# Staircase products, sums of groups and logits of an attention kernel moved into one step at one tile size, and output transposes moved beside those of keys

## The chip, the cores and the metric

The kernel runs on one core of a Trainium2 chip (trn2). The metric is the device time of one execution in microseconds (us). The core has a matrix engine (PE, with its weight loads shown apart as PEld), a vector engine (DVE), a scalar or activation engine (ACT), a general engine (POOL) and a queue engine that issues most transfers (SP). Each engine takes its instructions strictly in the order of the program; engines wait for each other by semaphores.

## The reference, cut to what matters

```python
# attention, B=4, H=8, S=768, D=64, fp32; block 32, window 16
k_sum = k.reshape(B, H, nb, block, D).max(axis=3)      # 24 group keys
v_sum = v.reshape(B, H, nb, block, D).mean(axis=3)     # 24 group values
scores_l = scale * q @ k.T            # kept only where |i - j| < window
scores_s = scale * q @ k_sum.T + log(block)
a = softmax(concat([scores_l, scores_s]))
attn = a @ concat([v, v_sum])
# then x = attn as 3072 tokens of 512, a two-level top-1 router (4 groups of 4
# experts) and the chosen expert's relu(x @ w1) @ w2, weighted
```

## The kernel before, in words

The attention is done in 16 "pairs" (one batch, two heads; 4 batches of 4 pairs), each in three steps g0, g1, g2 of four query tiles of 64 rows; the loop over `n` runs 48 such steps and three more that drain it. The mixture of experts follows; its time is most of the run, and its first parts begin as soon as the last logits are there.

What a step issues, and in which order, is written out by hand in the table `PLAN` (L47 to L49), one list for each of g0, g1, g2. All engines take their instructions in that order:

- `s`, `e`: scores of the step (16 matmuls of 64x64 tiles into `ps_s`, then DVE adds the mask and takes the maximum into `ss` and `nm`, L747), and ACT's exponentials `pr` (L756). `e` of a step needs its `ss`.
- `t`, `v`: transposes of `pr` two steps old (PE, 128x128, into `ps_tr`; ACT copies `ptS`, L764) and, three steps old, products with the values `va` (PE, 128x64, into `ps_av`); DVE then makes the reciprocal `rs` (L778) and the output `xt` (L779).
- `p0` to `p4`: preparation of the next pair. `p0` and `p1` transpose the keys of its two heads (`kn`, PE, 128x128); of each, ACT copies one half into `kw` and DVE the other (both L716; for the pairs that `ACT_K1` names, 10 to 15, ACT copies both halves of the second head). `p2`, `p3` transpose the queries (`qn`), and ACT copies `qt` (L710, two copies each). `p4` is DVE alone: two copies of window edges inside `kw` (L724, L725), the maximum over groups `ks` (L727) and its copy into `kw` (L730). The scores of the next pair's g0 come behind it.
- `m0`, `m1`: group means of the values. `m0` is 12 matmuls with the matrix `stair`, which write four groups of 32 rows of a bank, so that the tile of the array is 64x32; DVE copies the result to `vp` (L683). `m1` is one matmul with `same` (128x32); DVE copies it to `vr` (L687), and POOL spreads it over the 12 tiles of `va` in six copies (L690). The next pair's `v` needs them. In PLAN `m0` works for the pair after the current one and `m1` for the current one.
- `l0` to `l3`: logits of a finished pair. `l0` transposes four tiles of `xt` (ACT copies `xT`), `l1` the last two (DVE copies `xT`; both L800), `l2` multiplies with `wcat` (128x32, into `ps_lg`), `l3` is DVE's part once in a batch. `l0` runs one pair behind, `l1` to `l3` two.

All transposes, `m0` and `m1` take their result bank from one ring, `ps_tr`, of three banks: each new use waits until the copy out of the third one before it has ended. Where the table puts a step therefore also sets which copy it waits for. From step 17 on, DVE work of the router (`ROUTE_AT`) is dealt out between DVE's instructions. Transfers of q, k, v are issued from SP one to three pairs ahead.

`qt`, `kw`, `va`, `vp` and `xT` name the tiles in all rows below; every matmul and transpose is recorded at L118, a helper, so that PE's instructions are told apart by their tiles.

Of the kernel before, what the change touches and what calls it, by code (L numbers as in the profile page):

```python
# [8 lines left out]
F32 = mybir.dt.float32  # L9
# [12 lines left out]
B, H, S, D = 4, 8, 768, 64  # L22
# [6 lines left out]
NBLK = S // BLOCK  # L29
QT = 64  # L30
RUN = 8
NQT = S // QT

KW = QT + 2 * PAD
# [9 lines left out]
EPS = 1e-9  # L44
NEG = -1.0e9

PLAN = [["s", "p0", "t", "p1", "v", "m1", "l1", "e", "p4"],  # L47
        ["s", "p2", "t", "v", "l2", "e"],
        ["s", "p3", "l3", "t", "v", "m0", "l0", "e"]]  # L49
LAG = {"l0": 1, "l1": 2, "l2": 2, "l3": 2}  # L50

T_LAG, V_LAG = 2, 3
# [33 lines left out]
class Clock:  # L86

    pe, dve = float("-inf"), 0.0
    step = 0
# [452 lines left out]
def attention(tc, q, k, v, w_group, w_expert, ident, x_dram, ps, router, hook):  # L542
# [24 lines left out]
    with ExitStack() as st, ExitStack() as nat_st:  # L567
        cst = st.enter_context(tc.tile_pool(name="a_cst", bufs=1))
# [5 lines left out]
        order = [(b, a) for b in range(B) for a in range(NP)]  # L574
# [35 lines left out]
        t = ps_lg.next()  # L610
# [16 lines left out]
        def init_last(i):  # L627

            nc.gpsimd.memset(va_ring[i][96:NR, :, :, 0:D], 0.0)
# [33 lines left out]

        stair = cst.tile([QT, 2 * NBLK + 6], F32, name="stair")
        V.memset(stair, 0.0)
        for i in range(2):
            V.memset(stair[BLOCK * i:BLOCK * i + BLOCK, NBLK - 2 + i:NBLK - 1 + i], 1.0 / BLOCK)
# [3 lines left out]
        def means(idx, part):  # L673

            va = va_ring[idx % NVA]
            t = ps_tr.next()
            if part == 0:
                for i in range(NQT):
                    j = i % 4
                    T.matmul(out=t[32 * j:32 * j + 32, 0:P], lhsT=stair[:, NBLK - 2 - 2 * i:NBLK + 30 - 2 * i],  # L680
                             rhs=va[0:QT, i, :, 0:D], start=(i < 4), stop=(i >= NQT - 4), skip_group_check=True)
                vps[idx] = sm.tile([P, P], F32, name="vp", bufs=2)
                V.tensor_copy(out=vps[idx], in_=t[:, 0:P])  # L683
            else:
                T.matmul(out=t[KW:NC, 0:P], lhsT=same, rhs=vps.pop(idx), start=True, stop=True)
                vr = wk.tile([NC, 1, 2, D], F32, name="vr")
                V.tensor_copy(out=vr[KW:NC].rearrange("p a h d -> p (a h d)"), in_=t[KW:NC, 0:P])  # L687
                n = 2
                for i in range(0, NQT, n):
                    nc.gpsimd.tensor_copy(out=va[KW:NC, i:i + n, :, 0:D], in_=vr[KW:NC].broadcast_to([NBLK, n, 2, D]))  # L690
# [41 lines left out]
        def scores(n):  # L732

            idx, g = n // 3, n % 3
            qt, kw = qts[idx % 2], kws[idx % 2]
            sp = [ps_s.next()[:, 0:2 * NC].rearrange("p (j c) -> p j c", j=2) for _ in range(2)]
            for j in range(2):
                for i, h in ((0, 0), (1, 1), (1, 0), (0, 1)):
                    t, rows = 4 * g + 2 * j + i, slice(64 * h, 64 * h + 64)
                    T.matmul(out=sp[h][64 * i:64 * i + 64, j], lhsT=qt[rows, t].rearrange("p j r -> p (j r)"),  # L740
                             rhs=kw[rows, t], start=True, stop=True, skip_group_check=True)
            nm = sm.tile([P, 4], F32, name="nm")
            ss = sm.tile([P, 4, NC], F32, name="ss", bufs=2)
            for h in range(2):
                for j in range(2):
                    u, t = 2 * h + j, 4 * g + 2 * j
                    V.tensor_tensor_reduce(out=ss[:, u], in0=mask[:, 1 if t == 0 else 2 if t == NQT - 2 else 0],  # L747
                                           in1=sp[h][:, j], scale=1.0, scalar=3.4e38, op0=ALU.add, op1=ALU.min,
                                           accum_out=nm[:, u:u + 1])
            advance(OPS["s"][g])  # L750
            return ss, nm

        def exps(n, sp, nm):
            pr = prr[n % 3]
            for i in range(4):
                nc.scalar.activation(out=pr[:, i, 0:NC], in_=sp[:, i], func=AF.Exp, bias=nm[:, i:i + 1], scale=-1.0)  # L756
            return pr

        def transpose_p(pr):
            pt = ps_tr.next()  # L760
            for i in range(4):
                T.transpose(out=pt[0:NR, i * P:(i + 1) * P], in_=pr[:, i], identity=ident)
            ptS = wk.tile([NR, 4, P], F32, name="ptS", bufs=3)
            nc.scalar.copy(out=ptS.rearrange("p a c -> p (a c)"), in_=pt[0:NR])  # L764
            return ptS
# [20 lines left out]
        def store():  # L786
            b, js = stores.pop(0)
            nc.sync.dma_start(out=x_dram[b * S:(b + 1) * S].rearrange("(j r) d -> r j d", r=P)[:, js], in_=xs[b][:, js])
# [52 lines left out]
        for n in range(NG + 3):  # L841
            idx, g = n // 3, n % 3
            if n < NG:
                b, a = order[idx]
                xs[b] = x_ring[b % 2]
            for step in PLAN[g]:
                if step == "s" and n < NG:
                    sps = scores(n)
                elif step == "e" and n < NG:
                    prs[n] = exps(n, *sps)  # L850
                elif step == "t" and 0 <= n - T_LAG < NG:
                    pts[n - T_LAG] = transpose_p(prs.pop(n - T_LAG))
                elif step == "v" and 0 <= n - V_LAG < NG:
                    values((n - V_LAG) // 3, (n - V_LAG) % 3, pts.pop(n - V_LAG))
                elif step[0] == "p" and n < NG and idx + 1 < len(order):
                    prep(idx + 1, int(step[1]))
                elif step[0] == "m" and n < NG:
                    j = idx + (step == "m0")
                    if 0 < j < len(order):
                        means(j, int(step[1]))  # L860
                elif step[0] == "l" and 0 <= idx - LAG[step] < len(order):
                    logits(idx - LAG[step], int(step[1]))
            if n == 0:
                for i in range(1, NVA):
                    init_last(i)
                router.consts()
            elif n < 3:
                means(0, n - 1)
            if n in ROUTE_AT:
                b1 = ROUTE_AT.index(n)  # L870
                work.append(router.route(b1 * TB, (b1 + 1) * TB))
                if b1 == 1:
                    work.append(router.first_blocks())
            if n == NG - 4:
                nat_st.close()
            if n < NG:
                if g == 0 and 0 < idx < len(order) - 3:
                    qk[idx + 3] = load_qk(idx + 3)
                if g == 0 and idx + 2 < len(order):
                    load_vw(idx + 2)  # L880
            if g == 1 and stores:
                store()
            while stores and n == NG - 5:
                store()
            clock.step += 1
            hook(n, need, w1_first)
# [422 lines left out]
```

## Time and profile before

| | |
|---|---|
| median of 3 runs | 574.27 us (572.64 to 576.89) |
| profiled execution, own time | 573.17 us |
| span in its profile | 571.5 us |
| PE, DVE, ACT, POOL busy | 92%, 66%, 59%, 22% of the span |
| attention loop, first g2 of the pairs at | 17.85 us (pair 0) to 174.65 us (pair 14) |

In the rows a line of the timeline is start, busy time, engine, line of the code, operation, output tile<-input tiles, shape of output<-input and how many instructions the row joins; in brackets the idle time of the engine ahead of it and what ended it. A line of windows gives, for a stretch, its length and the busy time of each engine with its instruction count, then the granted clock of PE (1.00 is the full 2.4 GHz, 0.50 is 1.2 GHz), the DMA share and GB/s.

### The profile page before, as it was taken

What the parts mean: (1) busy time and instruction counts of PE and PEld (TensorE: products, weight loads), DVE (VectorE), ACT (ScalarE), POOL (GpSimd) and SP (SyncE); (2) the same over time, 40 slices, a digit from 0 to 9 for tenths busy, and PEclk for the clock granted to TensorE, in tenths of its full rate; (3) what the DMA queues carried; (4) which work ended last, traced back from release to release, by engine and by line L of the source; (5) the groups of instructions that cost most, each with busy time, mean ns of one, the idle gap of its engine ahead of it and who ended that gap; (6) DMA issues with size and microseconds to landing.
All of it is one profiled execution on the core that took longest, in us unless ns stands there. A gap on an engine that the chain in (4) does not pass through costs nothing.

```text
span 571.5 us, 13028 instructions
## 1 busy us (share of the span) xinstructions
PE 523.0 (92%) x4810; PEld 438.9 (77%) x4810; DVE 378.4 (66%) x1085; ACT 335.9 (59%) x615; POOL 123.9 (22%) x191
## 2 busy tenths in 40 slices
PE   6989888898999797998999999999999999979990
PEld 3766666676766676897998989989899898968880
DVE  7677788878885748855746547465484564738891
ACT  4577877798885714105635546445464464648880
POOL 7221122113113300125021302212022021222221
PEclk7599999999997889998999999999999999999996
DMA  9998776788655530399656665575656666558610
GB/s 156 190 188 158 132 149 153 159 147 191 115 134 198 176 121 0 122 394 357 225 187 217 253 243 204 174 254 221 239 204 218 235 217 234 192 190 289 225 22 22
DMA packets 72658, 107.24 MB, mean 188 GB/s; under 512 B 40366, under 2 KB 40446, under 8 KB 68736
## 3 DMA queue, kind: packets, MB, share of 16 engines
q1 hardware_dynamic: 66400, 88.88, 56.3%
q0 software_dynamic: 5120, 15.25, 7.3%
q10 hardware_dynamic: 1056, 2.10, 1.1%
q8 instruction: 42, 0.69, 0.5%
q14 instruction: 40, 0.33, 0.2%
HBM read 102.01 MB, written 13.63 MB: 202 GB/s over the span
## 4 chain that ended last, share of the span: by engine, by line
PE 53%; DVE 16%; issue 13%; DMA 8%; ACT 5%; POOL 1%; ACTq 0%; POOLq 0%; DVEq 0%
PE ps_s L118 31%; PE ps_av L118 11%; PE ps_tr L118 10%; DMA ohr<-x_dram,t_unit_gather 4%; DVE ks L727 2%; ACT pr L756 2%; DMA out_dram<-y,t_unit_scatter 2%; DVE ss L747 2%; ACT kw L716 1%; DVE kw L716 1%; DMA xg<-x_dram,t_unit_gather 1%; DVE xT L800 1%; DVE kw L725 1%; DVE kw L730 1%; DVE w1l L118 1%
## 5 line engine op out<-in xcount | busy, mean ns | idle before, releaser
L118 DVE TENSOR_TENSOR w2l<-w2r,w2h 128x1024 fp32r<-128x1024 f32 x60 | 73.0, 1224 | 79.3 <-ACT w2h L983 79.0
L118 PE MATMUL ps_s<-xT,w1h 128*128 128x256 f32 x448 | 87.3, 291 | 1.5 <-DVE hTl L118 1.5
L1025 POOL DMA_INDIRECT out_dram<-y,t_unit_scatter x24 | 30.3, 1262 | 223.1 <-ACT y L1020 151.3
L118 PEld LDWEIGHTS ps_s<-xT,w1h 128*128 128x128 f32 x448 | 73.3, 197 | 3.1 <-DVE hTl L118 1.7
L118 DVE TENSOR_TENSOR w1l<-w1r,w1h 128x1024 fp32r<-128x1024 f32 x60 | 69.5, 1220 | 6.4 <-ACT w1h L983 6.4
L756 ACT ACTIVATE pr<-ss,nm 128x120 f32<-128x120 f32 x192 | 60.1, 385 | 14.2 <-DVE nm L747 13.8
L983 ACT CAST w2h<-w2r 128x1024 fp32r<-128x1024 f32 x60 | 61.9, 1041 | 7.2 <-DVE w_all L118 4.5
L118 PE MATMUL ps_s<-xT,w1l 128*128 128x256 f32 x224 | 64.5, 288 | 0.0
L690 POOL COPY va<-vr 24x256 f32<-24x256 f32 x96 | 36.1, 420 | 127.6 <-DVE vr L687 127.6
L1063 ACT ACTIVATE hTh<-ps_s 128x512 fp32r<-128x512 f32 x48 | 28.7, 597 | 59.0 <-PE ps_s L118 38.9
L983 ACT CAST w1h<-w1r 128x1024 fp32r<-128x1024 f32 x60 | 58.4, 1046 | 0.0
L118 PE MATMUL ps_s<-ohr,w1h 128*128 128x256 f32 x320 | 58.1, 280 | 0.0
L118 PE MATMUL ps_s<-kw,qt 64*64 64x120 f32 x768 | 40.8, 294 | 12.2 <-DVE nm L747 10.2
L118 DVE SCALAR_TENSOR_TENSOR hTl<-ps_s,hTh 128x512 fp32r<-128x512 f32 x48 | 33.1, 690 | 26.8 <-ACT hTh L1063 26.8
L747 DVE CUSTOM_DVE_ANT_0 ss<-mask,ps_s 128x120 f32<-128x120 f32 x192 | 42.0, 273 | 11.8 <-PE ps_s L118 10.6
L118 PEld LDWEIGHTS ps_s<-ohr,w1h 128*128 128x128 f32 x320 | 49.5, 188 | 0.2
L118 PEld LDWEIGHTS ps_s<-kw,qt 64*64 64x64 f32 x768 | 24.9, 143 | 27.6 <-DVE nm L747 14.5
L118 PE MATMUL ps_av<-w2h,hTh 128*128 128x512 f32 x112 | 44.8, 400 | 0.0
L118 PE MATMUL ps_s<-ohr,w1l 128*128 128x256 f32 x160 | 44.7, 279 | 0.0
L118 PE MATMUL ps_s<-w2h,hTh 128*128 128x512 f32 x112 | 44.6, 398 | 0.0
L118 PEld LDWEIGHTS ps_s<-xT,w1l 128*128 128x128 f32 x224 | 44.2, 197 | 0.2
L118 PE MATMUL ps_av<-w2h,hTl 128*128 128x512 f32 x112 | 44.2, 395 | 0.0
(239 smaller groups left out, 1071.2 us busy)
## 6 DMA issues: line engine op xcount, KB each, us to landing
w1r<-in_moe_w_dram SPq DMA_DIRECT2D x32, 1024.0 KB
w2r<-in_moe_w_dram SPq DMA_DIRECT2D x32, 1024.0 KB
kn<-in_k_dram SPq DMA_DIRECT2D x16, 384.0 KB
qn<-in_q_dram SPq DMA_DIRECT2D x16, 384.0 KB
va<-in_v_dram SPq DMA_DIRECT2D x32, 192.0 KB
x_dram<-xt SPq DMA_DIRECT2D x12, 512.0 KB
va<-in_v_dram SPq DMA_DIRECT2D x64, 44.0 KB
w_first<-in_moe_w_dram SPq DMA_DIRECT2D x2, 1024.0 KB
```

Of the source, the lines that this page charges most:

```text
L118: return f(*args, **kw)
L690: nc.gpsimd.tensor_copy(out=va[KW:NC, i:i + n, :, 0:D], in_=vr[KW:NC].broadcast_to([NBLK, n, 2, D]))
L716: (nc.scalar.copy if j == 0 or h and idx in ACT_K1 else V.tensor_copy)(out=out[:, j], in_=tv.rearrange("p i t r -> p t r i"))
L725: V.tensor_copy(out=kw[:, 0:NQT - 1, behind], in_=kw[:, 1:NQT, 0:PAD])
L727: V.reduce_max(out=ks, axis=AX.X, in_=kw[:, :, 0:QT].rearrange("p t (a k) -> p t a k", k=BLOCK))
L730: V.tensor_copy(out=kw[:, :, KW:NC], in_=ks[:, None, :].broadcast_to([P, NQT, NBLK]))
L747: V.tensor_tensor_reduce(out=ss[:, u], in0=mask[:, 1 if t == 0 else 2 if t == NQT - 2 else 0], in1=sp[h][:, j], scale=1.0, scalar=3.4e38, ...
L756: nc.scalar.activation(out=pr[:, i, 0:NC], in_=sp[:, i], func=AF.Exp, bias=nm[:, i:i + 1], scale=-1.0)
L800: (V.tensor_copy if part else nc.scalar.copy)(out=xTs[idx][:, j0:j0 + n].rearrange("p c r -> p (c r)"), in_=tp[:, 0:n * P])
L983: (copy or self.nc.scalar.copy)(out=h, in_=src)
L1025: self.nc.gpsimd.indirect_dma_start(out=self.out, out_offset=bass.IndirectOffsetOnAxis(ap=self.tabs[name, "scatter"][:, col:col + 1], axis=0),
L1063: nc.scalar.activation(out=th[:, js], in_=hp, func=AF.Relu)
```

## The change

Three things. The matrix `stair` is made with `KW` = 96 rows (the added 32 are zero) in place of `QT` = 64, and the matmuls of `m0` read 96 rows of `va`, so that their tile is 128x32 like those of `same` and `wcat`. In PLAN, `l1` moves ahead of `t` in g0 to stand behind `p0`; `m1` moves from g0 to g1 and `m0` from g2 to g1, around `l2`. And `m0` of pair 1, which has no earlier place, is made with the first pair's means in step 2.

```diff
-PLAN = [["s", "p0", "t", "p1", "v", "m1", "l1", "e", "p4"],
-        ["s", "p2", "t", "v", "l2", "e"],
-        ["s", "p3", "l3", "t", "v", "m0", "l0", "e"]]
+PLAN = [["s", "p0", "l1", "t", "p1", "v", "e", "p4"],
+        ["s", "p2", "t", "v", "m1", "l2", "m0", "e"],
+        ["s", "p3", "l3", "t", "v", "l0", "e"]]
...
-        stair = cst.tile([QT, 2 * NBLK + 6], F32, name="stair")
+        stair = cst.tile([KW, 2 * NBLK + 6], F32, name="stair")
...
-                             rhs=va[0:QT, i, :, 0:D], start=(i < 4), stop=(i >= NQT - 4), skip_group_check=True)
+                             rhs=va[0:KW, i, :, 0:D], start=(i < 4), stop=(i >= NQT - 4), skip_group_check=True)
...
-                    if 0 < j < len(order):
+                    if 1 < j < len(order) or (j, step) == (1, "m1"):
                         means(j, int(step[1]))
...
             elif n < 3:
                 means(0, n - 1)
+                if n == 2:
+                    means(1, 0)
```

On PE, from `p0` in g0 of a pair to its products with values; the number behind `ps_tr` is the bank. Before:

```order
L118 MATMUL ps_tr_64<-ident,kn 128x96 x4
L118 MATMUL ps_tr_65<-ident,pr_187 121x128 x4
L118 MATMUL ps_tr_63<-ident,kn 128x96 x4
L118 MATMUL ps_av_69<-va_108,ptS 64x65 x8
L118 MATMUL ps_tr_64<-vp,same 24x128
L118 MATMUL ps_tr_65<-ident,xt_112 128x128 x2
```

And of the changed kernel, the same place:

```order
L118 MATMUL ps_tr_64<-ident,kn 128x96 x4
L118 MATMUL ps_tr_65<-ident,xt_112 128x128 x2
L118 MATMUL ps_tr_63<-ident,pr_187 121x128 x4
L118 MATMUL ps_tr_64<-ident,kn 128x96 x4
L118 MATMUL ps_av_69<-va_108,ptS 64x65 x8
```

The second transposes of keys (`p1`) stood in bank 63, whose user before them was three uses back in the step before; now they stand in bank 64, that of `p0`, and wait for DVE's copy of `p0`.

On PE, from the transposes of `pr` in g1 to the transposes of `xt` in g2 (the 8 + 8 single score matmuls between are left out here). Before, the end of g1 and the rest of g2:

```order
L118 MATMUL ps_tr_65<-ident,pr_188 121x128 x4
L118 MATMUL ps_av_69<-va_111,ptS 64x65 x8
L118 MATMUL ps_lg_70<-xT,wcat 32x192 x4
L118 MATMUL ps_s_67<-kw_134,qt_132 64x120
L118 MATMUL ps_tr_63<-ident,qn 128x96 x4
L118 MATMUL ps_tr_64<-ident,pr_186 121x128 x4
L118 MATMUL ps_av_69<-va_111,ptS 64x65 x8
L118 MATMUL ps_tr_65<-va_109,stair 32x128 x12
L118 MATMUL ps_tr_63<-ident,xt_112 128x128 x4
```

Of the changed kernel:

```order
L118 MATMUL ps_tr_64<-ident,pr_188 121x128 x4
L118 MATMUL ps_av_69<-va_111,ptS 64x65 x8
L118 MATMUL ps_tr_65<-vp,same 24x128
L118 MATMUL ps_lg_70<-xT,wcat 32x192 x4
L118 MATMUL ps_tr_63<-va_109,stair 32x128 x12
L118 MATMUL ps_s_67<-kw_134,qt_132 64x120
L118 MATMUL ps_tr_64<-ident,qn 128x96 x4
L118 MATMUL ps_tr_65<-ident,pr_186 121x128 x4
L118 MATMUL ps_av_69<-va_111,ptS 64x65 x8
L118 MATMUL ps_tr_63<-ident,xt_112 128x128 x4
```

`same`, `wcat` and `stair` now stand in one run ahead of g2's scores; `stair` takes bank 63 of `p2`, the transposes of `pr` in g2 take the bank of `same`, and those of `xt` the bank of `stair`.

On DVE, from the first copy of keys to the copy of group maxima. Before:

```order
L716 COPY kw_135<-ps_tr_65 64x12x32
L716 COPY kw_135<-ps_tr_64 64x12x32
L778 RECIPROCAL rs<-ps_av_69 128x4
L779 TENSOR_TENSOR xt_112<-ps_av_69,rs 128x2x128
L687 COPY vr<-ps_tr_65 24x128
L800 COPY xT<-ps_tr_63 128x256
L724 COPY kw_135<-kw_135 128x11x16
L725 COPY kw_135<-kw_135 128x11x16
L727 TENSOR_REDUCE ks<-kw_135 128x24
L730 COPY kw_135<-ks 128x12x24
```

Of the changed kernel:

```order
L716 COPY kw_135<-ps_tr_65 64x12x32
L800 COPY xT<-ps_tr_63 128x256
L716 COPY kw_135<-ps_tr_65 64x12x32
L778 RECIPROCAL rs<-ps_av_69 128x4
L779 TENSOR_TENSOR xt_112<-ps_av_69,rs 128x2x128
L724 COPY kw_135<-kw_135 128x11x16
L725 COPY kw_135<-kw_135 128x11x16
L727 TENSOR_REDUCE ks<-kw_135 128x24
L730 COPY kw_135<-ks 128x12x24
```

The copy of `xT` now stands between the two copies of keys, and that of `vr` has gone to the step before the scores of g2, with POOL's six copies behind it.

## Rows read from the trace of the kernel before

**Rows 1.** Windows, one pair each, from g2's scores to the next g2's scores.

```profile
42.00:53.19 11.19, 9.97 (x165) 7.40 (x165) 8.28 (x40) 8.71 (x23) 2.20 (x6) 1.00 1.07 176
75.56:87.44 11.88, 9.97 (x165) 7.40 (x165) 9.65 (x47) 8.70 (x23) 2.20 (x6) 1.00 0.73 161
110.59:120.77 10.18, 9.72 (x164) 7.34 (x164) 7.87 (x40) 9.10 (x24) 2.20 (x6) 1.00 0.80 136
142.54:153.12 10.58, 9.72 (x165) 7.34 (x165) 9.46 (x50) 9.21 (x24) 2.20 (x6) 1.00 0.77 145
```

**Rows 2.** Timeline of the pair from 42.00 to 53.19 us: its chain over the engines.

```profile
42.00 0.63 PE L118 MATMUL ps_s<-kw,qt 64*64 64x120 f32 x14 [0.70 <-DVE nm L747]
...
44.12 0.86 PE L118 MATMUL ps_tr<-va,stair 64*32 64x128 f32 x24
...
44.91 0.66 PE L118 MATMUL ps_tr<-ident,xt 128*128 128x128 f32 x4
...
45.61 0.58 ACT L800 COPY xT<-ps_tr 128x512 f32<-128x512 f32 x1 [0.86 <-PE ps_tr L118]
...
47.24 0.49 ACT L716 COPY kw<-ps_tr 64x384 f32<-64x384 f32 x1
...
47.76 0.56 DVE L716 COPY kw<-ps_tr 64x384 f32<-64x384 f32 x1 [0.58 <-ACT kw L716]
48.22 0.49 ACT L716 COPY kw<-ps_tr 64x384 f32<-64x384 f32 x1
...
48.75 0.56 DVE L716 COPY kw<-ps_tr 64x384 f32<-64x384 f32 x1 [0.42 <-ACT kw L716]
...
50.01 0.30 DVE L687 COPY vr<-ps_tr 24x128 f32<-24x128 f32 x1
...
50.34 0.42 DVE L800 COPY xT<-ps_tr 128x256 f32<-128x256 f32 x1
50.37 2.20 POOL L690 COPY va<-vr 24x256 f32<-24x256 f32 x6 [8.98 <-DVE vr L687]
50.68 0.25 DVE L724 COPY kw<-kw 128x176 f32<-128x176 f32 x1
50.85 0.45 DVE L725 COPY kw<-kw 128x176 f32<-128x176 f32 x1
...
52.19 0.55 DVE L730 COPY kw<-ks 128x288 f32<-128x288 f32 x1
...
53.19 0.63 PE L118 MATMUL ps_s<-kw,qt 64*64 64x120 f32 x14 [0.70 <-DVE nm L747]
```

**Rows 3.** The same timeline: PE with and without a change of tile.

```profile
42.95 0.62 PE L118 MATMUL ps_tr<-ident,pr 128*121 128x128 f32 x4
...
43.51 0.69 PE L118 MATMUL ps_av<-va,ptS 121*64 121x65 f32 x16
...
46.46 0.62 PE L118 MATMUL ps_tr<-ident,pr 128*121 128x128 f32 x4
...
46.92 0.50 PE L118 MATMUL ps_tr<-ident,kn 96*128 96x96 f32 x4
...
48.38 0.40 PE L118 MATMUL ps_tr<-vp,same 128*24 128x128 f32 x2 [0.35 <-DVE kw L716]
```

**Rows 4.** Timelines elsewhere: the copies of L725 and L730 without POOL's beside them.

```profile
15.46 0.24 DVE L725 COPY kw<-kw 128x176 f32<-128x176 f32 x1
...
86.69 0.30 DVE L730 COPY kw<-ks 128x288 f32<-128x288 f32 x1
```

**Rows 5.** Timeline of the pair from 142.54: ACT's copies of queries in g1.

```profile
151.08 0.98 ACT L710 ACTIVATE qt<-ps_tr 64x384 f32<-64x384 f32 x2
```

**Rows 6.** Windows of 2 us and PE's timeline near the loop's end.

```profile
174.00:176.00 2.00, 0.80 (x16) 0.57 (x16) 1.97 (x16) 1.29 (x5) 0.00 (x0) 1.00 1.04 404
...
178.00:180.00 2.00, 2.00 (x34) 1.63 (x37) 0.59 (x3) 1.33 (x3) 0.00 (x0) 0.51 0.09 34
...
179.25 1.50 PE L118 MATMUL ps_tr<-va,stair 64*32 64x128 f32 x24
```

## The prediction

> **What bounds the kernel now.** I read the windows first, one pair of the attention loop each [rows 1]. A plain pair lasts 11.19 us and keeps PE busy for 9.97, DVE for 8.28, ACT for 8.71: no engine is full, so a chain that crosses engines sets the period. Where the router's DVE work is dealt in (75.56 to 87.44) DVE is busy 9.65 of 11.88. From pair 10 on, ACT takes one of DVE's key copies: without router work the period is 10.18 with PE busy 9.72 and ACT 9.10, with router work 10.58 with DVE busy 9.46. So there are three kinds of pair with different limits, and I cost the change in each.
>
> The timeline of the plain pair shows its chain [rows 2]. I cut it at three rows, counting from g2's scores at 42.00:
> - Leg 1, 3.61 us: PE works in order through g2 (scores, queries, `t`, `v`, `stair` at 44.12, transposes of `xt` at 44.91), and ACT waits 0.86 for these transposes before it starts `xT` at 45.61.
> - Leg 2, 3.14 us: ACT, in its order, does `xT`, exponentials, the key copy at 47.24, `ptS`, the key copy at 48.22, and DVE, idle 0.58 and 0.42 ahead of its own halves, starts the second at 48.75.
> - Leg 3, 4.44 us: DVE runs without a pause through `rs`, `xt`, `vr` (50.01), `xT` (50.34), the three copies and the maximum of `p4`, and the mask of g2's scores; PE starts the bulk of these at 53.19 after 0.70 idle on DVE.
>
> The three make 11.19.
>
> **The change in a plain pair.** *Leg 1.* `stair` leaves the way to `xt`: 44.91 - 44.12 = 0.79 less. Against that stand two new waits: `t` in g2 takes the bank of `same` and so waits for DVE's `vr`, and the transposes of `xt` take the bank of `stair` and wait for `vp`. Behind them on PE are `v`, `l0` and the next scores. From the order and these durations I put `t` 0 to 0.3 us later, so `xT` starts 0.4 to 0.7 earlier, at 2.9 to 3.2 after g2's scores.
>
> *Leg 2.* ACT's first key copy moves from 5.24 (47.24 - 42.00) to 4.5 to 4.85, and DVE's half, 0.52 behind and 0.56 long, ends at 5.6 to 5.9 (before: 6.32). Here the change pays for itself: `p1` takes the bank of `p0` and PE cannot start it before that end, while before it started at 4.92 (46.92, [rows 3]). Behind it on PE stand `v` of g0 and the scores of g1; ACT's copy of `p1` and DVE's half follow 0.6 and 1.1 later. DVE's second half thus starts at 6.85 to 7.1, against 6.75: leg 1's gain is eaten and 0.1 to 0.35 more.
>
> *Leg 3.* Four things leave it. `vr` goes to g1 (50.34 - 50.01 = 0.33), `xT` moves ahead into DVE's wait for ACT (50.68 - 50.34 = 0.34; cover: the 0.42 idle; without that cover it would come back whole). And POOL's six copies, which now start at 50.37 just behind `vr` and run 2.20 us beside `p4`, move to g2: L725 takes 0.45 beside them and 0.24 without, L730 0.55 and 0.30 [rows 2, 4], so 0.21 + 0.25 = 0.46. Together 1.13; leg 3 becomes 3.31. That the 0.46 is POOL's doing is inferred from two rows each; bounds are 0 and 0.46, and I take 0.46, since rows with and without differ by about a factor of two.
>
> The Trainium skill (SBUF — State Buffer, section "SBUF: two separate sides") has VectorE and GpSimd share one port pair as an exclusive lock, so that the one waits for the other's whole instruction. By that rule the cost could be up to one POOL copy (2.20 / 6 = 0.37) on each of the two copies, 0.73 a pair, and the plain pairs would gain about 1.1 more in sum than I put. The rows show 0.46, and I stay with them.
>
> The DVE chain is then about 6.97 + 3.31 = 10.28: 0.9 less than 11.19. PE must follow. From `p1` at 46.92 to the next bulk of scores at 53.19 PE takes 6.27, with 0.35 idle before `same` [rows 3] and 0.70 before the scores; without these 5.22. In the changed order the transposes of `l1` no longer stand there (about 0.4, by the busy time of `same` beside them) and `stair` does (0.79), less three changes of tile. What a change of tile costs: from `pr` to `kn`, the same tile, 46.92 - 46.46 = 0.46; from `pr` to `av` 43.51 - 42.95 = 0.56; so 0.10 each, and PE's order has 14 changes a pair before and 11 now. That gives 5.3, from 5.85 on: 11.15, an upper end, since an idle time is counted from the modelled end of the matmul before it and each wait hides a few tenths besides. Taking those off (about 0.25 at each of three waits, one more ahead of `t`) gives 10.3. So a plain pair lies between 10.3 and 11.15; I take 10.3, -0.9.
>
> **The other pairs.** *Router work without ACT's extra copy (three pairs):* DVE is the limit there, leg 3 loses the 0.46, but `xT` and `vr` only change place, since DVE has little idle time to fill. -0.4 each; bounds 0 and -0.9.
>
> *ACT's extra copy, no router (one pair):* DVE is not late here, so its gains buy nothing, and `p1`'s wait falls on PE and ACT: ACT's double copy starts 0.2 to 0.3 later, then exponentials and the queries' copies (0.98 for two, [rows 5]); `stair` takes the bank of those and waits for their end. That chain gives about 10.6: +0.45.
>
> *ACT's extra copy and router work (five pairs):* between the two, 0 each; bounds -0.1 and +0.3.
>
> *Start and tail.* The first pair, at a lower clock, I give -0.5 (0 to -0.9). At the end, the last `stair` now runs in the step before 174.65 and not at 179.25, where the granted clock is 0.51 and it takes 1.50 in place of 0.86 [rows 2, 6]. PE is busy 2.00 of 2.00 there, so up to 1.5 comes off; since the work behind it is a chain over other engines I take -0.8 (bounds 0 and -1.4).
>
> The 32 added zero rows of `stair` I cost at nothing: four transposes over 121 rows take 0.62 and four over 128 rows 0.66 [rows 2, 3], so more rows add at most 0.04 to four matmuls, 0.1 to the twelve. They make `stair` wait for the borders of `va` too, whose transfers SP issues with the rest a pair or more ahead; if one came late, PE would stand with g2's scores behind it.
>
> **Sum.** 4 plain pairs x -0.9 = -3.6; 3 x -0.4 = -1.2; +0.45; 0; -0.5; -0.8: -5.65 us. The profiled execution took 573.17, so 567.5; the median of the runs lies 1.1 higher (574.27), so 568.6. With all the upper bounds (plain pairs -0.05, router 0, +0.45, 5 x 0.3, start and tail 0) it is +1.75, 576.0; with the lower ones about -10, 564.
>
> **The rivals.** A measurement of this kernel can tell about 1%, 5.7 us, from no change.
>
> *A, the sum above*, 565.5 to 571.5, chance 0.50. It lies on that border, so half of it counts as faster.
>
> *B, the copies of `p4` don't get shorter* (they are slow for another reason, or POOL's copies hit other DVE work in g2): 0.46 in each of seven pairs comes back, 568.6 + 3.2 = 571.8. For it: one row each without POOL. Chance 0.20.
>
> *C, PE is the bound and each change of tile that is saved comes off whole, with the waits covered:* 3 x 16 = 48 changes fewer at 0.10 = 4.8, with the gain of leg 3 (1.13 in four plain pairs, 4.5) beside it: 574.3 - 9.3 = 565. Against it: PE idles 1.2 of 11.19 now. Chance 0.12. The Trainium skill (TensorEngine Tiling (Array Packing), section "Key Properties") says that a change of the tiling mode drains the engine, which is this rival's mechanism; it names no price, and the rows give 0.10.
>
> *D, slower: the granted clock falls in the loop.* PE will stand for about 1.0 us ahead of `p1` and up to 0.3 ahead of `t`, in each pair, where its longest pause in the plain pair is now 0.70 at a granted clock of 1.00 [rows 1, 2]. Near the tail, PE is busy 0.80 of 2 us at a clock of 1.00 and two windows on the clock is 0.51 [rows 6]. One fall would cost some 2 us: the low stretch there is several us long, `stair` takes 1.50 for 0.86 in it, less the slack of a pair. It decides from three falls on, when the gain is gone; with six, 568.6 + 12 = 581. Against it: the loop has held 1.00 through gaps of this order in sum. The Trainium skill (TensorE: Matmul & The Clock Gate, section "What's actually happening") says that the low clock is the default and activity lifts it, which speaks for this rival; no run here yet shows where it tips. Chance 0.12.
>
> *E, nothing moves*: gains in the plain pairs are lost again to `t`'s and `p1`'s waits: 574. Chance 0.06.
>
> **The numbers.** Faster by over 1%: half of A and C, about 0.38. Within 1%: the other half of A, B, E, 0.50. Slower: D, 0.12. The range 564.0 to 576.0 holds A, B, E and most of C; D lies outside.
>
> **What would show it.** Right: plain pairs near 10.3; L725 and L730 at 0.24 and 0.30; POOL's copies right after g2's scores; PE idle about 1 us ahead of `p1`, ended by DVE's copy of keys; pair 10 slower than 10.18; no `stair` at a low clock near the end. Wrong: granted clock under 1.00 between 30 and 170 us (D), the two copies as long as before (B), no idle time ahead of `p1` (C).

## The result

The changed kernel takes 568.62 us (median of 4 runs, 567.45 to 569.19) beside 575.58 (572.64 to 578.14) for the kernel before; the ratio is 0.9899 with a 95% interval of 0.9862 to 0.9936. The profiled execution took 568.16 with a span of 566.4, so 5.0 us less than the one the sum was made against. The time forecast was 568.6. The sum behind it was not as good as that: the start came out 3.4 us longer than its terms say, and the tail and other terms made up for it.

Windows of the changed kernel, columns as in [rows 1]: first the pairs that answer to those rows, then the two at the start.

```profile
54.30:64.61 10.31, 9.22 (x165) 7.46 (x165) 7.84 (x40) 8.59 (x24) 2.13 (x6) 1.00 0.74 136
...
74.93:85.92 10.99, 9.64 (x167) 7.64 (x166) 9.35 (x45) 8.41 (x23) 2.13 (x6) 1.00 0.80 174
...
107.95:119.11 11.16, 9.82 (x166) 7.59 (x165) 8.55 (x49) 9.55 (x25) 2.13 (x6) 1.00 0.68 127
...
140.70:151.24 10.54, 9.43 (x168) 7.41 (x165) 9.20 (x50) 9.12 (x24) 2.13 (x6) 1.00 0.72 144
...
16.88:32.14 15.26, 10.38 (x163) 8.12 (x160) 7.61 (x42) 9.05 (x25) 4.27 (x12) 0.84 1.17 211
32.14:43.98 11.84, 10.75 (x167) 8.84 (x164) 6.96 (x35) 7.69 (x20) 0.00 (x0) 0.83 1.12 183
```

The plain pair fell from 11.19 to 10.31, a pair with router work from 11.88 to 10.99, the pair with ACT's extra copy and no router work rose from 10.18 to 11.16, and one with both stayed (10.58 and 10.54). The first two periods are longer than before (12.95 and 11.20 there), at a mean clock of 0.84 and 0.83. Before it was 0.61 and 1.00, so it is not the clock that makes the first of them longer.

The timeline of the pair from 54.30 answers to [rows 2]:

```profile
54.30 0.64 PE L118 MATMUL ps_s<-kw,qt 64*64 64x120 f32 x16
...
54.87 0.55 PE L118 MATMUL ps_tr<-ident,qn 96*128 96x96 f32 x4
55.03 0.30 DVE L687 COPY vr<-ps_tr 24x128 f32<-24x128 f32 x1
...
55.38 0.70 PE L118 MATMUL ps_tr<-ident,pr 128*121 128x128 f32 x4
55.39 2.13 POOL L690 COPY va<-vr 24x256 f32<-24x256 f32 x6 [8.18 <-DVE vr L687]
...
57.32 0.59 ACT L800 COPY xT<-ps_tr 128x512 f32<-128x512 f32 x1 [0.27 <-PE ps_tr L118]
...
59.46 0.56 DVE L716 COPY kw<-ps_tr 64x384 f32<-64x384 f32 x1 [0.57 <-ACT kw L716]
60.05 0.42 DVE L800 COPY xT<-ps_tr 128x256 f32<-128x256 f32 x1
...
60.08 0.55 PE L118 MATMUL ps_tr<-ident,kn 96*128 96x96 f32 x4 [1.09 <-DVE kw L716]
...
61.20 0.56 DVE L716 COPY kw<-ps_tr 64x384 f32<-64x384 f32 x1 [0.72 <-ACT kw L716]
...
62.52 0.24 DVE L725 COPY kw<-kw 128x176 f32<-128x176 f32 x1
...
63.30 0.29 PE L118 MATMUL ps_tr<-vp,same 128*24 128x128 f32 x1
...
63.65 0.31 DVE L730 COPY kw<-ks 128x288 f32<-128x288 f32 x1
63.66 0.29 PE L118 MATMUL ps_tr<-va,stair 96*32 96x128 f32 x3
...
64.61 0.64 PE L118 MATMUL ps_s<-kw,qt 64*64 64x120 f32 x16
```

`xT` starts 3.02 behind g2's scores (before 3.61), `p1` waits 1.09 for DVE's copy of `p0`, DVE's second half starts 6.90 behind (before 6.75), L725 takes 0.24 and L730 0.31, POOL's copies lie in g2, and from the second half to the next scores it is 3.41 (before 4.44). The three lengths are close to those that were worked out, but the last leg no longer closes on DVE alone. PE has no idle time in its rows from `p1` at 60.08 to the scores at 64.61, which is 4.53 of the 10.31; DVE's chain comes back only through `vr`, for which the transposes of `pr` wait (they stand 0.51 behind those of the queries, without such a wait 0.38). The two paths nearly tie.

The start did not. PE's rows there:

```profile
30.59 1.62 PE L118 MATMUL ps_tr<-va,stair 96*32 96x128 f32 x24 [4.68 <-DMA va<-in_v_dram]
32.14 1.08 PE L118 MATMUL ps_s<-kw,qt 64*64 64x120 f32 x16
```

The `stair` of pair 2, which now stands in g1, waits 4.68 us for that pair's values, and behind the wait PE runs at half clock (16 score matmuls take 1.08, in the loop 0.64).

### The profile page after: what moved, and what is told of

Read it like the earlier page. It is cut to its first block, busy times and chain, and to the rows that moved or that the text cites. A ratio compares the mean times of both kernels' runs of the same rounds, so it can differ in the third digit from the quotient of the medians.

```text
span 566.4 us, 13048 instructions
## 1 busy us (share of the span) xinstructions
PE 512.9 (91%) x4810; PEld 438.0 (77%) x4810; DVE 371.7 (66%) x1085; ACT 335.0 (59%) x615; POOL 123.2 (22%) x191
## 4 chain that ended last, share of the span: by engine, by line
PE 56%; issue 12%; DVE 12%; DMA 10%; ACT 5%; POOL 1%; SPq 1%; ACTq 0%; POOLq 0%; DVEq 0%
PE ps_s L118 32%; PE ps_av L118 13%; PE ps_tr L118 10%; DMA ohr<-x_dram,t_unit_gather 4%; ACT pr L756 3%; DMA out_dram<-y,t_unit_scatter 2%; DMA va<-in_v_dram 2%; DVE ss L747 1%; DVE kw L716 1%; DVE xt L779 1%; DMA xg<-x_dram,t_unit_gather 1%; SPq L599 1%; DVE w1l L118 1%; ACT kw L716 1%; PE ps_lg L118 1%
## 5 line engine op out<-in xcount | busy, mean ns | idle before, releaser
L118 PE MATMUL ps_s<-xT,w1h 128*128 128x256 f32 x448 | 85.9, 288 | 1.5 <-DVE hTl L118 1.5
L118 PEld LDWEIGHTS ps_s<-xT,w1h 128*128 128x128 f32 x448 | 72.0, 194 | 2.9 <-DVE hTl L118 1.7
L118 PE MATMUL ps_s<-w2l,hTh 128*128 128x512 f32 x112 | 44.2, 395 | 0.0
L118 PE MATMUL ps_av<-w2l,hTh 128*128 128x512 f32 x112 | 44.2, 395 | 0.0
L118 PE MATMUL ps_s<-w2h,hTl 128*128 128x512 f32 x112 | 44.2, 395 | 0.0
```

Of the source, the lines that this page charges most:

```text
L118: return f(*args, **kw)
```

## The experiments

Periods below are those of plain pairs in the middle of the loop, read from one g2's scores to the next; the pair shown is a typical one. In some runs a single pair is longer by 0.5 to 2.8, with a stop of PE or a stretch at half clock in it. The ratios are to the kernel before, whose median lay between 573.38 and 575.53 us in these runs.

**One part undone: the tile of `stair`.**

```diff
-        stair = cst.tile([KW, 2 * NBLK + 6], F32, name="stair")
+        stair = cst.tile([QT, 2 * NBLK + 6], F32, name="stair")
...
-                             rhs=va[0:KW, i, :, 0:D], start=(i < 4), stop=(i >= NQT - 4), skip_group_check=True)
+                             rhs=va[0:QT, i, :, 0:D], start=(i < 4), stop=(i >= NQT - 4), skip_group_check=True)
```

> The changed kernel with one part undone: the staircase matrix has 64 rows again, so its tile is 64x32 and stands as a different tile between the logits and the scores. Theory A (the order of waits made the gain; a change of tile costs about 0.1 us): same, logits and stair take 1.31 us to the next scores in a plain pair of the changed kernel; here about 1.45 to 1.6, the plain period goes from 10.3 to 10.4 to 10.6, and the whole to about 570 to 572. Theory C (tile changes carry the gain): the plain period goes back above 10.9 and the whole to about 573. The 4.68 us wait for the values of pair 2 gets shorter here, since stair reads only the rows that land first: by both theories up to 2 us come off at the start, which is kept apart by reading the plain periods.

564.35 us (ratio to before 0.983, 0.9794 to 0.9866): 4.3 us below the change as a whole, though the two intervals just touch. Window of a plain pair, and PE's rows from its timeline, with the wait at the start first:

```profile
61.08:71.40 10.32, 9.22 (x168) 7.30 (x164) 7.83 (x42) 8.81 (x24) 2.14 (x6) 1.00 0.73 134
...
28.86 0.86 PE L118 MATMUL ps_tr<-va,stair 64*32 64x128 f32 x24 [0.94 <-DMA va<-in_v_dram]
...
59.63 0.29 PE L118 MATMUL ps_tr<-vp,same 128*24 128x128 f32 x1
...
60.29 0.86 PE L118 MATMUL ps_tr<-va,stair 64*32 64x128 f32 x24
61.08 0.64 PE L118 MATMUL ps_s<-kw,qt 64*64 64x120 f32 x16
61.65 0.55 PE L118 MATMUL ps_tr<-ident,qn 96*128 96x96 f32 x4
62.03 0.69 PE L118 MATMUL ps_tr<-ident,pr 128*121 128x128 f32 x4
```

From `same` to g2's scores it is now 61.08 - 59.63 = 1.45, in the changed kernel 64.61 - 63.30 = 1.31. So the common tile is worth 0.14 a pair on PE. The period shows none of it (10.32 and 10.31): in the changed kernel the transposes of `pr` stand 0.51 behind those of `qn` (54.87 to 55.38), with the other tile 0.38, since DVE's `vr`, for which they wait, comes at its own time. Rival C falls. What the tile does cost is at the start: with 64 rows `stair` waits for the values alone, and the wait is 0.94 and not 4.68. `stair` starts 1.73 earlier (28.86 and 30.59); the rest of the shorter wait is that PE comes to it 2.0 later (its first stretch at half clock lasts until 24.6 here and until 19.0 there). Behind the long wait the changed kernel has a second such stretch (29.3 to 36.1), which this one hasn't. The g2 of pair 2 starts at 39.90 in place of 43.98.

**The tile alone, in the kernel before.** The same two lines, the other way round, and no move.

> The kernel before with the 96 rows of stair alone; the order of steps stays. Its tile becomes 128x32, but it still stands between products with values (128x64) and transposes (128x128), so the number of tile changes stays. Theory A: plain period 11.19 plus at most 0.1, no wait for values at the start, where stair of pair 2 stands at 32.9; the whole within 1.5 us of the kernel before. Rival: the tile of its own is worth something, and the whole falls by 2 us or more.

572.00 us, ratio 0.999 (0.9964 to 1.0017): no difference. The plain pair:

```profile
53.75:64.95 11.20, 9.97 (x164) 7.40 (x164) 8.28 (x40) 8.71 (x23) 2.20 (x6) 1.00 0.78 125
...
44.69 0.86 PE L118 MATMUL ps_tr<-va,stair 96*32 96x128 f32 x24
45.48 0.66 PE L118 MATMUL ps_tr<-ident,xt 128*128 128x128 f32 x4
```

The 96 rows themselves cost nothing: `stair` takes 0.86, with 0.79 to the next, as in [rows 2].

**One part alone: `m1`.**

```diff
-PLAN = [["s", "p0", "t", "p1", "v", "m1", "l1", "e", "p4"],
-        ["s", "p2", "t", "v", "l2", "e"],
+PLAN = [["s", "p0", "t", "p1", "v", "l1", "e", "p4"],
+        ["s", "p2", "t", "v", "m1", "l2", "e"],
```

> The kernel before with one part of the change alone: m1 (sums of groups, the copy vr and POOL's copies) moved from g0 to the place ahead of the logits in g1; stair with 64 rows, m0 and l1 stay. Theory A: 0.33 of vr and 0.46 of L725 and L730 leave the end of DVE's chain, and p1 has no new wait; the plain period falls from 11.19 to 10.4 to 10.7, L725 takes 0.24 and L730 0.31, and the whole falls to 564 to 569. Rival B (POOL's copies are not what makes the two slow): L725 stays at 0.45 and L730 at 0.55, and the plain period falls by no more than 0.35, the whole stays above 570.

559.61 us, ratio 0.9731 (0.9666 to 0.9796), better than the whole change and below the range that was given, as is the plain period. The plain pair, with rows of POOL and DVE in it:

```profile
49.27:59.57 10.30, 9.59 (x165) 7.41 (x165) 7.84 (x40) 8.62 (x23) 2.13 (x6) 1.00 0.95 180
...
50.56 2.13 POOL L690 COPY va<-vr 24x256 f32<-24x256 f32 x6 [8.16 <-DVE vr L687]
...
56.02 0.56 DVE L716 COPY kw<-ps_tr 64x384 f32<-64x384 f32 x1 [0.43 <-ACT kw L716]
...
57.67 0.24 DVE L725 COPY kw<-kw 128x176 f32<-128x176 f32 x1
...
58.80 0.31 DVE L730 COPY kw<-ks 128x288 f32<-128x288 f32 x1
```

The second half of the keys starts 56.02 - 49.27 = 6.75 behind g2's scores, as before; from there to the next scores it is 3.55 and not 4.44. All of the 0.89 is in that leg: `vr` (0.33) and POOL's copies (0.46) have left it, and with `vr` a gap of 0.10 ahead of it. Nothing waits at the start, and the pair with ACT's extra copy and no router work takes 9.53 where the changed kernel takes 11.16.

**POOL's copies put back beside `p4`.** Added work in the changed kernel, from pair 3 on:

```diff
+                for _ in range(8 if idx > 2 else 0):
+                    junk = sm.tile([P, 4, D], F32, name="junk", bufs=1)
+                    nc.gpsimd.tensor_copy(out=junk[KW:NC], in_=kw[KW:NC, 0:4, 0:D])
```

> The changed kernel with added work: eight copies on POOL, of the size of those into va (24x256), that read the keys and write a scratch tile and start with p4, from pair 3 on. Theory A (POOL's copies make L725 and L730 slow): L725 goes from 0.24 to 0.4 to 0.45, L730 from 0.31 to 0.45 to 0.6, the plain period from 10.3 to 10.5 to 10.8, less what PE's own order covers, and the whole to 571 to 575. Rival B: both copies keep their lengths, and the whole stays within 1 us of 568.6.

571.79 us, ratio 0.9966 (0.9929 to 1.0004), 3.2 above the changed kernel, though the two intervals just touch. The plain pair, and rows of POOL and DVE in it (three lines further down in this kernel, so that L733 is the copy of L730 and L730 the maximum of L727):

```profile
53.47:64.22 10.75, 9.49 (x166) 7.64 (x165) 8.23 (x40) 8.59 (x22) 5.37 (x15) 1.00 0.77 130
...
61.55 3.71 POOL L728 COPY junk<-kw 24x256 f32<-24x256 f32 x8 [4.42 <-DVE kw L716]
...
62.01 0.25 DVE L724 COPY kw<-kw 128x176 f32<-128x176 f32 x1
62.17 0.45 DVE L725 COPY kw<-kw 128x176 f32<-128x176 f32 x1
62.54 0.93 DVE L730 TENSOR_REDUCE ks<-kw 128x24 f32<-128x768 f32 x1
...
63.51 0.55 DVE L733 COPY kw<-ks 128x288 f32<-128x288 f32 x1
```

The two copies are back at 0.45 and 0.55, the very lengths of [rows 2], and the period is 0.44 longer. The copy of L724 and the maximum beside the same copies of POOL keep theirs here. Rival B falls, and the 0.46 that was inferred from two rows each is shown for the plain pair.

**One part alone: `l1` behind `p0`.**

```diff
-PLAN = [["s", "p0", "t", "p1", "v", "m1", "l1", "e", "p4"],
+PLAN = [["s", "p0", "l1", "t", "p1", "v", "m1", "e", "p4"],
```

> The kernel before with one part of the change alone: l1 moved from the end of g0 to behind p0; stair, same and logits stay where they were. Theory A: p1 then waits for DVE's copy of p0 (idle time of about 1.3 us ahead of p1), xT leaves the end of DVE's chain (0.34), and the copy of p1 is late by 0.6 to 0.9; the plain period is 11.2 to 11.6, the whole 574 to 580: alone this part costs. Rival: l1's move is what made the gain; the plain period falls below 10.9 and the whole below 571.

585.58 us, ratio 1.019 (1.015 to 1.023). The window and the wait:

```profile
42.53:54.26 11.73, 9.70 (x165) 7.36 (x165) 8.46 (x40) 8.71 (x23) 2.29 (x6) 1.00 0.81 155
...
48.89 0.55 PE L118 MATMUL ps_tr<-ident,kn 96*128 96x96 f32 x4 [1.09 <-DVE kw L716]
```

The sign and the mechanism were expected, the size was not: 0.54 a plain pair, against the 0 to 0.4 expected, and two of the pairs with router work came to 14.3. This is the first of them:

```profile
90.34:104.68 14.34, 12.86 (x171) 9.83 (x172) 9.71 (x50) 9.13 (x24) 2.36 (x6) 0.76 0.62 134
```

Its granted clock is 0.76, and so is that of the next; the pair ahead of them, with router work at a clock of 1.00, takes 12.64. PE had stood 1.83 and 1.48 us, waiting for DVE, just before each fall. This is rival D, in another kernel than the one it was put up for.

**`l1` put back, or put ahead of `p0`, in the changed kernel.**

```diff
-PLAN = [["s", "p0", "l1", "t", "p1", "v", "e", "p4"],
+PLAN = [["s", "p0", "t", "p1", "v", "l1", "e", "p4"],
```

Back to the end:

> The changed kernel with l1 put back to the end of g0; m0, m1 and the 96 rows stay as changed. Theory W (l1 behind p0 costs, by p1's wait for p0's bank, and m1's move alone made the gain): no idle time ahead of p1, xT back in DVE's chain (0.34); the plain period is 9.8 to 10.2, below the 10.31 of the changed kernel, and the whole falls to 562 to 566, since the wait at the start stays. Rival: l1's move contributes to the gain; the plain period rises to 10.4 or more and the whole to 570 or more.

559.87 us, ratio 0.9785 (0.9741 to 0.9829), below the 562 to 566 expected. The plain pair:

```profile
53.40:63.32 9.92, 9.39 (x166) 7.54 (x165) 7.74 (x42) 8.63 (x23) 2.13 (x6) 1.00 0.84 141
```

Ahead of `p0`, so that `p1` takes the bank of `l1`:

```diff
-PLAN = [["s", "p0", "l1", "t", "p1", "v", "e", "p4"],
+PLAN = [["s", "l1", "p0", "t", "p1", "v", "e", "p4"],
```

> The changed kernel with l1 issued ahead of p0 and not behind it, so that p1's transposes take the bank of l1's transposes of xt and wait for the copy of xT, not for DVE's copy of p0. Theory W (the wait of p1 on p0's bank holds the plain period at 10.3): the idle time ahead of p1 falls from 1.09 to below 0.5, ACT's copy of p1 starts right behind ptS, the plain period falls to 9.6 to 9.9 and the whole to 560 to 564. Rival X (ACT's own order sets the period, with p1 only waiting inside it): the idle time moves to another place on PE and the plain period stays at 10.2 to 10.3, the whole at 567 to 569.5.

559.95 us, ratio 0.9746 (0.9708 to 0.9783). Its plain pair and the wait of `p1`:

```profile
53.51:63.09 9.58, 9.28 (x165) 7.50 (x164) 7.74 (x42) 8.62 (x23) 2.14 (x6) 1.00 0.93 160
...
58.56 0.55 PE L118 MATMUL ps_tr<-ident,kn 96*128 96x96 f32 x4 [0.27 <-DVE xT L800]
```

So in a plain pair the same step costs 0.39 behind `p0` (9.92 to 10.31) and saves 0.34 ahead of it (9.92 to 9.58); the two places differ in the order of `l1` and `p0` and with it in the bank that `p1` takes. The whole does not show the 0.34 (559.95 and 559.87): over the six pairs with ACT's extra copy, from the g2 of pair 8 to that of pair 14, `l1` ahead of `p0` takes 61.33 and at the end 59.56.

**The start: the values of pair 2 loaded earlier.** In the changed kernel, `load_vw(2)` is issued ahead of `load_qk(3)`.

> The changed kernel with the loads of pair 2's values issued ahead of the loads of pair 3's queries and keys. Theory S (at the start PE idles 4.68 us on those values, because stair of pair 2 now stands at 25.9 us): the wait falls to 0 to 2.5 us, stair starts 2 to 4.5 us earlier, and the whole time falls by as much, to about 564 to 566.5. Rival: the transfers are bound by bandwidth at the start and the keys of pair 3 come late in turn; the wait only moves, and the time stays within 1 us of 568.6.

565.46 us (ratio 0.9846, 0.9795 to 0.9896), as expected, though the interval overlaps that of the changed kernel; and the profile shows a part of it moved. Rows of PE and the second window:

```profile
27.44 0.98 PE L118 MATMUL ps_tr<-va,stair 96*32 96x128 f32 x24 [0.52 <-DMA va<-in_v_dram]
...
36.91 1.08 PE L118 MATMUL ps_s<-kw,qt 64*64 64x120 f32 x15 [1.57 <-issue]
...
28.35:42.86 14.51, 11.85 (x167) 9.74 (x164) 8.59 (x41) 9.07 (x24) 3.13 (x9) 0.76 1.13 187
```

The wait falls from 4.68 to 0.52, and the g2 of pair 1 starts at 28.35 in place of 32.14. In the next pair PE stands 1.57 with nothing to wait for in the profile ("issue") and then runs at half clock, and of the 3.8 us 1.1 are left at the g2 of pair 2 (42.86 and 43.98).

**ACT's extra copy one pair later**, `ACT_K1 = range(11, B * NP)`:

> The changed kernel with ACT's extra key copy beginning one pair later, at pair 11, so that the one such pair without router work is an ordinary pair again. Theory A (in the changed order this pair pays for p1's wait on ACT, and the logits' stair waits for ACT's copies of queries): its period falls from 11.15 to 10.3 or 10.4, and the whole by about 0.8, to 567.5 to 568. Rival: its period is long for another reason (the batch's end, l3 and lT); then it stays above 10.9.

567.16 us, not to be told from the changed kernel by its interval (0.9799 to 0.9931). The pair takes 10.84: 0.32 of the 0.85 that was expected, so the rest has another cause. Which move brings it is told by other runs (below).

**The gains together.** The changed kernel with `l1` ahead of `p0` and 64 rows:

> The changed kernel with the two edits of the first runs that gained, l1 ahead of p0 and stair back at 64 rows. If the two act in different places (the one in every pair, the other at the start, by the wait for the values of pair 2), their gains add: plain period 9.5 to 9.7 and the whole 555 to 557. Rival: with p1's wait gone PE has less cover, the change of tile of 0.14 shows in each pair, and the whole is 557 to 559.5.

560.08 us (ratio 0.9723, 0.9649 to 0.9798): the plain period is 9.57 and the g2 of pair 14 starts at 163.32 (165.96 without the 64 rows), but the whole is that of the run without the 64 rows, in place of 555 to 557. One pair lasts 10.93, with a stop of PE in it:

```profile
52.24 0.49 PE L118 MATMUL ps_tr<-ident,qn 96*128 96x96 f32 x4 [1.47 <-issue]
```

And what is gained up to the g2 of pair 14 is lost behind it: 395.95 us from there to the end, and 392.71 in the run without the 64 rows. The kernel before with `m1` in g1 and `l1` ahead of `p0`:

> The kernel before with two moves: m1 ahead of the logits in g1, and l1 ahead of p0 in g0, so that p1 takes the bank of l1 and not that of p0. Stair keeps 64 rows and its place in g2. If both gains act apart (m1: plain period 10.3; l1 ahead: xT leaves the end of DVE's chain, 0.34, without p1 waiting on p0), the plain period is 9.9 to 10.0 and the whole 555 to 558. Rival: stair in g2 delays xT and with it ACT's chain, which now sets the period; it stays at 10.2 to 10.3 and the whole at 559 to 561.

561.07 us (ratio 0.9821, 0.9772 to 0.987); plain pair 9.95, as expected, the whole not. One pair of it has the same kind of stop as above, here in its profile:

```profile
38.65:48.60 9.95, 9.59 (x165) 7.45 (x165) 7.83 (x40) 8.58 (x23) 2.13 (x6) 1.00 1.25 178
...
48.60:61.33 12.73, 11.21 (x165) 8.71 (x165) 7.84 (x40) 8.83 (x23) 2.13 (x6) 0.87 1.04 164
...
52.01 0.22 PE L118 MATMUL ps_av<-va,ptS 121*64 121x65 f32 x1 [1.23 <-issue]
```

Last, each part only in the pairs where it gained:

```diff
+PLAN = [["s", "p0", "t", "p1", "v", "l1", "e", "p4"],
+        ["s", "p2", "t", "v", "m1", "l2", "e"],
+        ["s", "p3", "l3", "t", "v", "m0", "l0", "e"]]
+PLAN_MID = [["s", "l1", "p0", "t", "p1", "v", "e", "p4"],
+            ["s", "p2", "t", "v", "m1", "l2", "m0", "e"],
+            ["s", "p3", "l3", "t", "v", "l0", "e"]]
...
+            for step in (PLAN_MID if 2 <= idx < 9 else PLAN)[g]:
```

> The parts that gained, each where it gained. All pairs: m1 ahead of the logits in g1, stair with 64 rows. Pairs 2 to 8 besides: l1 ahead of p0, and m0 behind the logits in g1. At the start and in the pairs with ACT's extra copy, stair and l1 stay where they were before. If the parts act apart: plain period 9.6, the pairs with ACT's extra copy 9.5 to 10.3, no wait for values at the start, the g2 of pair 14 at 157 to 160 us, and the whole at 554 to 557. Rival: the work behind the attention (the first experts, at a lower clock in part) takes back what comes before 162 us, as it did between the runs so far, whose ends differ by less than their g2 of pair 14 do; the whole stays at 558 to 560.

557.60 us (median of 6 runs, 555.79 to 561.97), ratio 0.9707 (0.9665 to 0.975): 11 us below the changed kernel and the lowest median of all, though its interval overlaps those of the runs around 560. Plain pairs take 9.58 and those with ACT's extra copy 9.4 to 10.3, but the g2 of pair 14 starts at 161.01, above the 157 to 160 expected.

## Why the prediction came out right

The loop first. By the plain period:

| kernel | `m1` in | `m0` in | `l1` | plain pair, us | the six pairs with ACT's extra copy, us | whole, us |
|---|---|---|---|---|---|---|
| before | g0 | g2 | end | 11.19 | 64.06 | 575.58 |
| `m1` alone | g1 | g2 | end | 10.30 | 59.25 | 559.61 |
| `m1`, `m0`, 96 rows | g1 | g1 | end | 9.92 | 59.56 | 559.87 |
| changed | g1 | g1 | behind `p0` | 10.31 | 64.25 | 568.62 |
| the same, `l1` ahead of `p0` | g1 | g1 | ahead of `p0` | 9.58 | 61.33 | 559.95 |
| `l1` alone | g0 | g2 | behind `p0` | 11.73 | 69.94 | 585.58 |

The steps of the prediction for the plain pair hold, but for where leg 3 ends. *Leg 1*: `xT` 0.59 earlier (said: 0.4 to 0.7); it is `m0`'s move, worth 0.38 of the period where nothing eats it. *Leg 2*: `p1` waits 1.09 (about 1.0), the second half at 6.90 (6.85 to 7.1); the gain of leg 1 is eaten, as said, and the runs with `l1` elsewhere show that it was that bank. (As its rows add up, the range was 6.7 to 7.0.) *Leg 3*: 3.41 (3.31), closed by PE's order as much as by DVE, which the prediction had worked out beside it, with 10.3 as the result. The 0.46 of the rows was right, and the 0.73 a pair was not reached. The Trainium skill (SBUF — State Buffer, section "SBUF: two separate sides") has VectorE and GpSimd share a port pair as an exclusive lock. The longer copies agree with that, by 0.21 and 0.25 us, but no run shows that a lock is what makes them so. The waits on `vr` and `vp` in g2 cost about 0.1.

What the prediction did not see is how unlike the parts are. It summed one new order. The runs show one move with all of the net gain (`m1`), one with a gain that only shows without `l1` (`m0`), one that costs (`l1`, +10 us alone, of which some 3.4 lies in the two pairs at half clock: 14.34 and 14.33 beside 12.64), and one that does nothing in the loop and costs about 4 us at the start (the 96 rows).

The terms, with the changes of start times of g2's scores between the two profiles:

- Plain pairs: three with -0.9 each as said (-2.6 together); the fourth, from 30.80, lies in the disturbed start. The term is right for the three that were undisturbed.
- Router work (three pairs): -0.89, -0.60 and -0.52, -2.0 in place of -1.2. DVE had more idle time to fill than was said: it was busy 9.65 of 11.88 and is busy 9.35 of 10.99, and `m1` alone takes 2.3 off these three. Of the 0.46 only the 0.21 of L725 can be in it, since L730 took 0.30 in these pairs already (86.69 [rows 4]); for the same reason rival B's 0.46 in seven pairs was too much.
- ACT's extra copy without router work: +0.98 in place of +0.45. The sign was right. A third of it is that copy. By the moves: `m1` alone takes this pair from 10.18 to 9.53, `m0` with its rows brings it to 10.17, and `l1` behind `p0` to 11.16. Why `l1` costs 0.99 here and 0.39 in a plain pair is open.
- Both: -0.8 over five pairs in place of 0, from -0.48 to +0.30.
- These last two terms are near the mark by luck. The prediction counted no gain of `m1` in the first ("DVE is not late here, so its gains buy nothing") and none in sum in the others. By the table `m1` alone takes 4.8 off the six pairs, and `l1` behind `p0` puts 4.7 back.
- **Start: +2.0 at the g2 of pair 2 in place of -1.4 (-0.5, and -0.9 for the fourth plain pair). This is the step that failed.** The prediction wrote that the added rows "make `stair` wait for the borders of `va` too, whose transfers SP issues with the rest a pair or more ahead", and gave that no price. At the start nothing is a pair ahead: SP issues these transfers from 18.46 to 26.16 us, and PE comes to `stair` at 25.91. With 96 rows the wait is 4.68, with 64 it is 0.94, and in the old place `stair` waited for neither.
- Tail: -2.65 in place of -0.8, by the spans behind the g2 of pair 14 (396.85 and 394.2). `stair` has left the low stretch, as said. But the size is not `stair`'s alone: this stretch lasted from 391.9 to 399.3 in the profiles of all kernels here, not in the order of what was changed. It goes with the clock. In the 110 us behind that g2 the granted clock was 0.97 where the stretch lasted 391.9, 0.89 where it lasted 399.3, and before and in the changed kernel:

```profile
174.65:284.65 110.00, 99.48 (x792) 86.84 (x793) 71.12 (x233) 44.92 (x78) 21.11 (x22) 0.91 0.54 194
...
172.20:282.20 110.00, 99.01 (x786) 86.98 (x784) 74.08 (x232) 46.41 (x79) 23.28 (x28) 0.94 0.55 196
```

Over all fourteen profiles, one microsecond more at half clock there goes with some 0.4 us more to the end (an estimate, from a straight line through them). The kernel before spends 20.5 us at half clock there and the changed kernel 13.7. By that line the difference alone is worth 2.8, so the 2.65 can't be put down to `stair`. What makes the clock fall more or less there is open, and it is why gains of a few us before 165 us (the last runs) did not all reach the end.

The start (with the fourth plain pair in it) came out 3.4 higher than said, the tail 1.9 lower, the router and extra-copy terms -0.8, +0.5 and -0.8 off; so the sum came within 1 us of the time by cancelling, and that is luck. (The lower end of its range does not follow from its terms: their lower bounds add up to -8.65 and not -10, so to 565.6 and not 564.) Of the rivals, B is refuted by POOL's added copies, C by the tile that was undone, E by the table. D did not come in the loop of the changed kernel: `p1` pauses 1.09 to 1.11 in ten of the thirteen pairs from 32 us on, and the granted clock stayed 1.00 from 36 to 176 us. It did come once, behind the 4.68 us at the start, and in the loop of three of the other kernels: twice with `l1` alone behind `p0`, once with POOL's added copies (88.6 us) and once in the kernel before with `m1` and `l1` moved (53.0 us). The Trainium skill (TensorE: Matmul & The Clock Gate, section "What's actually happening") has the low clock as the default that activity lifts; the rows here agree in the one long pause.

## What to carry to other kernels

Cost a bundle of moves part by part, and ask of each what it does alone: here one of four moves gave more than the whole, and a step that was to share a tile size paid with a wait for data. When a step moves in a program with a short ring of banks, write down which copy each later user now waits for: one place up or down turned a loss of 0.39 into a gain of 0.34. Where the limit is another, as in the six pairs with ACT's extra copy, the same place can lose again. And check a move apart in the first rounds, where nothing has been loaded ahead yet.

## What was not expected of the hardware

A copy from SBUF to SBUF on DVE took 0.24 alone and 0.45 beside POOL's copies, and another 0.31 and 0.55; the copy of L724, of the same size as the first, and the maximum over 768 columns kept 0.25 and 0.93. Which copies are hit is not told by their size, and not by their line either: in the run with POOL's added copies, the first pair with them has L724 at 0.45 and L725 at 0.24 (40.57 and 40.94 us), and one later pair has both copies short beside them (0.24 and 0.30, at 108.98 and 110.35).

Matmuls of one tile size that write different columns of the array can run at the same time: `same` (rows 96 to 119 of its result) starts at 63.30 and the first logits (from row 0 on) at 63.31, as the timeline above and this row of the changed kernel show, where the kernel before has 0.33 from `same` to the next tile, of another size.

```profile
63.31 0.36 PE L118 MATMUL ps_lg<-xT,wcat 128*32 128x192 f32 x3
```

PE stood still three times with nothing in the profile that it waited for: 1.57 us in the run with earlier values, 1.23 in the kernel before with `m1` and `l1` moved, and 1.47 in the changed kernel with both gains. With two of the stops came a stretch at half clock, with the third (1.47) none, and 1.09 us in most pairs left the clock at 1.00; so the length of a pause alone does not tell. The traces show where the stops are. Counted over all of PE's records, weight loads included, PE stops behind the 705th in the first of these runs and behind the 1217th in the other two, 512 apart, although their orders differ; and each time a 16 KiB transfer of the queue that the profile calls `instruction` (q8) had landed 1.3 to 1.8 us before PE went on (at 35.6, 50.5 and 50.4 us). At the same two places the other kernels idle 0.6 at most, and there that transfer had landed 1.6 us or more before. This points to PE waiting for its own instructions. No run here tests it.
